# One core, three blocks: the values' product of windowed attention by blocks of 64 keys, its normalisation for the first sequence at the product's eviction, and the next sequence's first scores ahead of the low-rank stage

## The chip, the cores and the metric

The kernel runs on one core of a Trainium2 chip. The metric is the device time of one execution in microseconds, smaller is better. The engines are named as in the profile: PE (TensorE, matrix products and transposes), PEld (its weight loads), DVE (VectorE), ACT (ScalarE), POOL (GpSimd), SP (the queue that issues the DMAs). All operands stay in SBUF; PE writes to PSUM, eight banks of 512 float32 columns, from which DVE and ACT copy ("evict").

## The reference

Four sequences (`batch`) of 576 positions pass through three blocks.

```python
# 1 attention: 8 heads of width 64, window of 128 keys, linear bias
scores = q @ k.T / 8 + slope_h * -|i - j|          # only where 0 <= i - j < 128
attn = exp(scores - max); attn = attn / (sum(attn) + 1e-9)
x = concat_heads(attn @ v)                          # [4, 576, 512]
# 2 low rank mix over positions, then a feed-forward block (hidden 2048)
u = x + ((x.T @ U) @ V).T                           # rank 32, over the 576 positions
x = u + relu(u @ w_ch1) @ w_ch2
# 3 spatial gating
h = relu(x @ w_in); a, b = halves of h
b = layernorm(b); b = w_spatial @ b + b_spatial[:, None]
out = (a * b) @ w_out
```

The inputs U, V and the weight matrices come as 64-bit words of float64 values; the kernel takes them apart into float32 on the chip ("bit unpacking").

## The kernel before, in words

**Attention** is done for one sequence `b` and a pair of heads at a time (`heads`, 16 pairs in all). The 576 queries are cut into nine tiles `t` of 64; both heads of the pair stand in the 128 partitions, and a tile sees at most 192 keys. The steps of a pair:

1. scores on PE (L577, 18 products, in two groups of six and three tiles) into the PSUM ring `sc`;
2. on DVE, for each tile, the bias added and the row's negative maximum taken in one instruction (L589), result to SBUF `p`;
3. on ACT `exp` with the row sums (L594);
4. on DVE one add and one reciprocal for all nine tiles (L599, L601), then nine normalisations `p = p * rinv` (L607 on POOL or L609 on DVE, the planner takes the engine);
5. on PE transposes of `p`, 128x128 each (L616). The keys are cut at 0, 64, 192, 320, 448 (`CH`): a chunk `c` of keys is needed by up to four tiles (`TR`), which makes 17 transposes in five PSUM buffers, evicted to `ph` (L317 on ACT, L318 on DVE);
6. on PE the values' product (L639): 14 matrix products, seven per head, the two heads in the two column halves of the array, with 64 to 256 moving columns each (1088 per head), into two buffers for the query ranges 0 to 320 and 320 to 576; two copies to `u` (L317, L318).

After the fourth pair of a sequence: `u` is transposed (L659), mixed with U (L675), multiplied with V (L687), and added to `u` by eight DVE instructions (L692).

**The feed-forward block** goes over the hidden width in four quarters (`PARTS`) of four chunks of 128. Each operand is split into two float32r parts, so a product is three passes (L460 to L462 and L497 to L499). The first quarter's weights are loaded and unpacked during attention (`part_of_hidden`, DVE L362 to L369, ACT L356, POOL L384), eight of them. With them `NB` = 5 "early" groups of 256 tokens run on PE between the pieces of attention of sequences 1 to 3; all other token groups are "late", 512 tokens at a time (1024 tokens of the first quarter, then all 2304 for each other quarter). **The third block** follows; it is not touched.

**The order** on every engine is made by a planner (`Plan`): each step is a task with an estimated cost, a priority (pairs in order; weights by `K["w0"] + K["w0s"] * c`) and its dependencies, including those of the buffer rings; it lists tasks by the earliest possible start and the priority, and the engines run this list in order. A ring (`Ring`) hands out buffers in turn, in the order in which the Python code asks for them, so code that is written earlier gets its buffer earlier. `qr`, `kr` (queries, keys) have two buffers each, so a pair's load waits for the scores of the pair before the last. The attention's buffers (`att`) are given up for the late ones when all attention is done (`end_att`).

## Time and profile before

| | us |
|---|---|
| median of 3 runs (761.59 to 763.09) | 763.0 |
| the profiled execution | 763.91 |
| its span, first to last instruction | 762.1 |
| PE busy | 735.4 (96%) |
| DVE busy | 414.4 (54%) |
| ACT busy | 318.5 (42%) |
| POOL busy | 268.4 (35%) |

The profile is one execution, of one core. Busy time of PE counts a matrix product from its issue to its modelled end, and products overlap; so a duration there is latency, and the distance between the starts of two instructions is what one costs in a stream. Rows of DVE and ACT overlap by some 0.08 us for the same reason. A float32 product appears as two records, since it goes in two passes. The granted clock is a share of the full 2.4 GHz; the other level is 1.2 GHz.

### The profile page before, as it was taken

The numbers are of one execution on the slowest core, as the hardware profiler recorded it, in microseconds if no ns is written. First come the engines' busy times: TensorE is split into PE (matmuls) and PEld (weight loads), VectorE is DVE, ScalarE is ACT, GpSimd is POOL, SyncE is SP. The second block draws the span as 40 slices with busy tenths as digits, with TensorE's granted clock in tenths as the row PEclk, the third lists the DMA queues.
The fourth block names the chain that finished last, engine by engine and source line by source line (L and its number), as shares of the span: only waits on it lengthen the run. The fifth ranks groups of instructions, "written<-read, shape, count | busy, mean of one in ns | idle before, by whom it ended". The sixth has DMA issues, their size and how long they took to land.

```text
span 762.1 us, 13056 instructions
## 1 busy us (share of the span) xinstructions
PE 735.4 (96%) x4988; PEld 633.0 (83%) x4988; DVE 414.4 (54%) x1077; ACT 318.5 (42%) x856; POOL 268.4 (35%) x347
## 2 busy tenths in 40 slices
PE   6788999999989999999999999999999999999998
PEld 5567888888867888889888888888999899899897
DVE  5999767587499852225992164122685505415220
ACT  5867657485543432124541233122454333332322
POOL 1252231110455652124762136152386206115021
PEclk9999999999999999999999999999999999999999
DMA  6855213120424200006000030000310010100102
GB/s 210 261 174 174 91 32 110 50 79 2 138 99 139 83 1 1 0 1 221 1 0 1 1 112 0 1 1 0 111 48 1 15 43 1 42 28 1 55 2 69
DMA packets 28834, 45.70 MB, mean 60 GB/s; under 512 B 4964, under 2 KB 18020, under 8 KB 28772
## 3 DMA queue, kind: packets, MB, share of 16 engines
q1 hardware_dynamic: 28772, 44.87, 18.3%
q8 instruction: 39, 0.64, 0.4%
q14 instruction: 23, 0.19, 0.1%
HBM read 40.14 MB, written 4.72 MB: 59 GB/s over the span
## 4 chain that ended last, share of the span: by engine, by line
PE 87%; DVE 9%; ACT 1%; DMA 1%; issue 1%; SPq 0%; POOL 0%; ACTq 0%; DVEq 0%; POOLq 0%
PE sc L497 5%; PE sc L499 5%; PE sc L498 5%; PE at L460 5%; PE at L462 5%; PE at L461 5%; PE at L616 4%; PE acc L497 3%; PE at L639 3%; PE acc L499 3%; PE acc L498 3%; PE f L460 3%; PE at L791 3%; PE at L790 3%; PE at L789 3%; PE f L461 3%
## 5 line engine op out<-in xcount | busy, mean ns | idle before, releaser
L434 POOL TENSOR_TENSOR x<-u,xc 128x64 fp32r<-128x64 f32 (+5 forms) x108 | 92.9, 895 | 134.2 <-ACT xc L431 132.9
L469 DVE SCALAR_TENSOR_TENSOR h<-at,h 128x512 fp32r<-128x512 f32 (+1 forms) x51 | 32.7, 642 | 95.6 <-ACT h L467 95.6
L467 ACT ACTIVATE h<-at 128x512 fp32r<-128x512 f32 (+1 forms) x51 | 28.6, 560 | 125.0 <-PE at L462 124.9
L594 ACT ACTIVATE p<-p,nmax 128x192 f32<-128x192 f32 (+1 forms) x144 | 61.5, 432 | 8.8 <-DVE nmax L589 8.8
L616 PE MATMUL at<-ident,p 128*128 128x128 f32 x272 | 42.2, 300 | 5.8 <-DVE p L609 4.5
L589 DVE CUSTOM_DVE_ANT_0 p<-sc,bias 128x192 f32<-128x192 f32 (+1 forms) x144 | 39.9, 327 | 14.2 <-PE sc L577 14.0
L577 PE MATMUL sc<-kr,qr 64*64 64x192 f32 (+2 forms) x576 | 34.3, 335 | 11.9 <-DMA kr<-in_kT 4.6
L460 PE MATMUL at<-xc,wb 128*128 128x512 f32 (+1 forms) x120 | 44.2, 368 | 0.0
L497 PE MATMUL sc<-h,wb 128*128 128x512 f32 (+1 forms) x120 | 44.1, 368 | 0.0
L498 PE MATMUL sc<-h,wb 128*128 128x512 f32 (+1 forms) x120 | 44.1, 368 | 0.0
L462 PE MATMUL at<-x,wb 128*128 128x512 f32 (+1 forms) x120 | 44.1, 368 | 0.0
L461 PE MATMUL at<-xc,wb 128*128 128x512 f32 (+1 forms) x120 | 44.1, 368 | 0.0
L499 PE MATMUL sc<-h,wb 128*128 128x512 f32 (+1 forms) x120 | 44.1, 368 | 0.0
L384 POOL TENSOR_TENSOR wa<-st,wa 128x512 fp32r<-128x512 f32 x24 | 32.6, 1366 | 32.4 <-ACT wa L317 22.4
L616 PEld LDWEIGHTS at<-ident,p 128*128 128x128 f32 x272 | 33.7, 152 | 12.2 <-issue 4.1
L804 POOL TENSOR_TENSOR u<-y,u 128x576 fp32r<-128x576 f32 x16 | 24.0, 1517 | 53.6 <-ACT u L802 53.6
L469 DVE SCALAR_TENSOR_TENSOR h<-f,h 128x512 fp32r<-128x512 f32 (+1 forms) x27 | 17.8, 659 | 42.9 <-ACT h L467 42.8
L384 POOL TENSOR_TENSOR wb<-st,wb 128x512 fp32r<-128x512 f32 x20 | 30.7, 1546 | 28.3 <-ACT wb L317 28.3
L431 ACT CAST xc<-u 128x64 fp32r<-128x64 f32 (+5 forms) x108 | 38.3, 437 | 3.8 <-PE at L687 3.8
L577 PEld LDWEIGHTS sc<-kr,qr 64*64 64x64 f32 x576 | 22.1, 141 | 19.1 <-issue 15.7
L467 ACT ACTIVATE h<-f 128x512 fp32r<-128x512 f32 (+1 forms) x27 | 15.4, 571 | 53.2 <-PE f L462 52.1
L497 PE MATMUL acc<-h,wa 128*128 128x256 f32 (+1 forms) x108 | 35.9, 332 | 1.5 <-DVE y L507 1.2
(327 smaller groups left out, 2274.1 us busy)
## 6 DMA issues: line engine op xcount, KB each, us to landing
wa<-in_w SPq DMA_DIRECT2D x16, 512.0 KB, 5.4
wb<-in_w SPq DMA_DIRECT2D x16, 512.0 KB, 5.0
qr<-in_qT SPq DMA_DIRECT2D x16, 288.0 KB, 2.9
kr<-in_kT SPq DMA_DIRECT2D x16, 288.0 KB, 3.4
vr<-in_v SPq DMA_DIRECT2D x16, 256.0 KB, 2.8
wa<-in_w_in SPq DMA_DIRECT2D x8, 512.0 KB, 3.6
out<-h SPq DMA_DIRECT2D x15, 256.0 KB, 2.0
wb<-in_w_out SPq DMA_DIRECT2D x4, 512.0 KB, 4.3
```

Of the source, the lines that this page charges most:

```text
L384: P.add("POOL", pool_tt(k * c), lambda: nc.gpsimd.tensor_tensor(out=b[:, 1], in0=st.ap(), in1=f32(b[:, 0]), op=ALU.subtract), r=[st, b.par ...
L434: nc.gpsimd.tensor_tensor(out=tl[il][:, o : o + m], in0=ub[:, s : s + m], in1=f32(th[ih][:, o : o + m]), op=ALU.subtract)
L460: nc.tensor.matmul(o, wt[:, 0, k], a[ia], start=k == 0, stop=False)
L461: nc.tensor.matmul(o, wt[:, 1, k], a[ia], start=False, stop=False)
L462: nc.tensor.matmul(o, wt[:, 0, k], l[il], start=False, stop=k == 3)
L469: P.add("DVE", dve(per * n), lambda f1=f1, hh=hh, hl=hl: nc.vector.scalar_tensor_tensor(out=hl.ap(), in0=f1.ap(), scalar=0.0, in1=f32(hh.a ...
L497: nc.tensor.matmul(o, wt[:, 0, 0, c], hh[:, j], start=i == 0 and x == 0, stop=False, skip_group_check=True)
L498: nc.tensor.matmul(o, wt[:, 1, 0, c], hh[:, j], start=False, stop=False, skip_group_check=True)
L499: nc.tensor.matmul(o, wt[:, 0, 0, c], hl[:, j], start=False, stop=i == len(wts) - 1, skip_group_check=True)
L577: nc.tensor.matmul(s[o : o + 64, c0 : c0 + k1 - k0], qr[d, 64 * t : 64 * t + 64], kr[d, k0:k1], start=True, stop=True, skip_group_check=True)
L594: nc.scalar.activation(out=o(), in_=o(), func=AF.Exp, scale=-1.0, bias=nmax[:, sl, t : t + 1], accum_out=sums[:, sl, t : t + 1])
L616: P.add("PE", 0.109, lambda pt=pt, t=t, half=half, blk=blk: nc.tensor.transpose(pt[:, blk * 128 : blk * 128 + 128], p[:, t, half * 128 : h ...
```

## The change

1. **Values' product by 64-key blocks.** A slot of `p` is now 128 columns wide, 13 slots (`NP`) in place of 9 x 256 columns. For tile `t` the last 128 keys stand in one slot (`MAIN`) and the 64 keys before them in half of another (`REST`), so 13 transposes in four PSUM buffers (`GROUPS`, `SLOTS`) take the place of 17 in five; the evictions fall from 2176 to 1664 columns for each pair. The product is 32 matrix products of 64 moving columns: first eight tiles with all 128 rows (two heads in two column halves), then eight with 64 rows in quarters of the array; even and odd tiles go to two PSUM banks of 320 and 256 columns. The values lie in chunks of 128 keys; the zeroed buffers `v0` go.
2. **First sequence** (`plain`, `pn=1`). Its nine normalisations per pair go. In their place POOL makes `dg`, an identity times `rinv` (128x576); PE multiplies it with ones (four products, L659 of the new file), which brings `rinv` to the layout of the output; two ACT copies bring that to SBUF `r`; and the two copies of the product to `u` become two DVE multiplications with `r`. The other three sequences keep the nine normalisations.
3. **Next scores first.** `heads` is cut in two: loads, scores, maxima and `exp` of the next sequence's first pair are asked for ahead of `low_rank`.
4. **Numbers.** `qr`, `kr` get three buffers, `NB` goes from 5 to 6 early groups (1536 tokens; 768 of the first quarter are left for late groups, as 512 and 256), the first quarter's weights get earlier priorities (`w0` 8 to 7, `w0s` 1.23 to 0.6). V is unpacked in a 128x288 layout in place of 128x576 and spread to its four copies by four DMAs from SBUF to SBUF.

```diff
+GROUPS = [(2, 3), (4, 5), (6, 7), (8, 0, 1)]
...
-    r_qr, r_kr, r_vr, r_v0 = Ring(in_att, "qr", 2), Ring(in_att, "kr", 2), Ring(in_att, "vr", 3), Ring(in_att, "v0", 3)
-    r_ph = Ring(in_att, "ph", 6)
+    r_qr, r_kr, r_vr = Ring(in_att, "qr", K["nq"]), Ring(in_att, "kr", K["nq"]), Ring(in_att, "vr", 3)
+    r_ph = Ring(in_att, "ph", 2)
...
-        single(v32, [(0, stacked(block(V, 0, RANK, 0, S), 4))], 1, S, prio_v, None, early_v)
+        single(v4, [(0, stacked(block(V, 0, RANK, q * n, q * n + n), 2), slice(64 * q, 64 * q + 64)) for q in range(2)],
+               1, n, prio_v, None, early_v)
...
+            if plain:
+                dg = r_d.new([128, 9, D], F32)
+                P.add("POOL", pool_tt(S), lambda: nc.gpsimd.tensor_tensor(
+                    out=dg.ap(), in0=eye.ap().broadcast_to([128, 9, D]),
+                    in1=rinv[:, sl, :9].rearrange("p (t o) -> p t o", o=1).broadcast_to([128, 9, D]), op=ALU.mult),
+                    r=[rinv.part(sl), eye.part(0), eye.part(1)], w=[dg], prio=p0 + 4)
+            else:
...
+            for g, (s0, s1) in enumerate(SLOTS):
+                pt = tp.new([128, s1 - s0, 128], F32)
+                for n_ in range(s0, s1):
+                    ts = [t for t in range(9) if n_ in (MAIN.get(t), REST.get(t))]
+                    P.add("PE", 0.109, lambda pt=pt, n_=n_, s0=s0: nc.tensor.transpose(
+                        pt[:, n_ - s0], p[:, n_ * 128 : n_ * 128 + 128], ident), ...)
+                copy(engines("e", "ACT"), 128 * (s1 - s0), lambda s0=s0, s1=s1: x[:, s0:s1], pt.ap, PSUM, ...)
...
+                            if where is MAIN:
+                                rows, c = slice(0, 128), (t - 1) // 2
+                            else:
+                                rows, c = slice(64 * e, 64 * e + 64), (t - 2 * e) // 2
...
+                                nc.tensor.matmul(os_[e][j * 64 : j * 64 + 64, k], vr[rows, j, c], x[rows, where[t], swap : swap + 64],
+                                                 start=(e, j) not in started, stop=last, skip_group_check=True)
...
+            if plain:
+                for e in range(2):
+                    P.add("DVE", dve(D * (5 - e)), lambda e=e: nc.vector.tensor_tensor(
+                        out=view(e), in0=os_[e].ap(), in1=r[:, e::2], op=ALU.mult), r=[r.part(e), os_[e]], w=[ub.part(e)], prio=p0 + 9)
...
-            heads(b, pair)
+            (heads(b, pair) if pair or not b else ahead)()
...
+        if b < B - 1:
+            ahead = heads(b + 1, 0)
         low_rank(b, xts)
...
-K = dict(parts=(4, 4, 4, 4), flex='xeht', cp=0, wp=0, low=6, w0=8, w0s=1.23, nb=5, evac=40.0, nst=3, d0=7, d0s=0.91, lowd=5)
+K = dict(parts=(4, 4, 4, 4), flex='xeht', cp=0, wp=0, low=6, w0=7, w0s=0.6, nb=6, evac=40.0, nst=3, d0=7, d0s=0.91, lowd=5, nq=3, pn=1)
```

How the order changes, at three places. On DVE, behind the first pair's `exp`: the first pair of the first sequence and the beginning of the second pair, before (`p_77`, `p_81` are the two buffers `p`; L609 normalises, L589 takes the maxima):

```order
L599 TENSOR_SCALAR rinv<-sums 128x9
L601 RECIPROCAL rinv<-rinv 128x9
L609 TENSOR_SCALAR p_77<-p_77,rinv 128x64
L609 TENSOR_SCALAR p_77<-p_77,rinv 128x128
L609 TENSOR_SCALAR p_77<-p_77,rinv 128x192 x7
L589 ISA p_81,nmax<-sc,bias 128x64
```

and the same place of the changed kernel (`p_86` the second buffer, L613 the maxima):

```order
L327 COPY ph<-at 128x384
L559 MEMSET u_127 64x32
L624 TENSOR_SCALAR rinv<-sums 128x9
L626 RECIPROCAL rinv<-rinv 128x9
L613 ISA p_86,nmax<-sc,bias 128x64
```

The nine normalisations are gone from between the reciprocal and the next pair's maxima, and two evictions of transposed tiles stand ahead of the reciprocal.

On PE, the second pair of the second sequence, before (L616 transposes, L639 the values' product, L659 the transposes of `u`, L577 scores; `v_533` is a buffer `v0`):

```order
L616 MATMUL at<-ident,p_81 128x128 x2
L639 MATMUL at<-ph,v_533 64x64 x2
L639 MATMUL at<-ph,v_533 64x128 x2
L639 MATMUL at<-ph,vr 64x256 x2
L639 MATMUL at<-ph,vr 64x128 x4
L639 MATMUL at<-ph,vr 64x256 x2
L639 MATMUL at<-ph,vr 64x128 x2
L659 MATMUL at<-ident,u 128x128 x4
```

and in the changed kernel (L602 scores, L648 transposes, L686 the values' product, L713 the transposes of `u`):

```order
L602 MATMUL sc<-kr,qr 64x64 x2
L602 MATMUL sc<-kr,qr 64x128 x2
L602 MATMUL sc<-kr,qr 64x192 x8
L648 MATMUL at<-ident,p_86 128x128 x12
L686 MATMUL at<-ph,vr 64x64 x32
L713 MATMUL at<-ident,u 128x128 x10
```

One product of 32 steps with 64 columns stands in place of 14 in six rows, behind 13 transposes (one is further up) in place of 17.

On DVE, where the early groups end and the weights of the second quarter are unpacked, before (`st` are weights; L469 makes the second part of a hidden chunk, which PE waits for):

```order
L362 TENSOR_SCALAR st<-st 128x512
L363 TENSOR_SCALAR st<-st 128x512
L366 SCALAR_TENSOR_TENSOR st<-wb,st 128x512
L362 TENSOR_SCALAR st<-st 128x512
L369 SCALAR_TENSOR_TENSOR st<-wb,st 128x512
L363 TENSOR_SCALAR st<-st 128x512
L469 SCALAR_TENSOR_TENSOR h<-at,h 128x512
```

and in the changed kernel, from the first weight on (L372 to L379 unpack, L517 adds to `y`, L479 makes the hidden chunk's part):

```order
L372 TENSOR_SCALAR st<-st 128x512
L373 TENSOR_SCALAR st<-st 128x512
L376 SCALAR_TENSOR_TENSOR st<-wb,st 128x512
L517 TENSOR_TENSOR y<-acc,u 128x128 x4
L379 SCALAR_TENSOR_TENSOR st<-wb,st 128x512
L372 TENSOR_SCALAR st<-st 128x512
L479 SCALAR_TENSOR_TENSOR h<-f,h 128x512
```

The same passes come first, but the chunk behind them now belongs to the sixth early group: on PE, 72 products of early groups follow the last low-rank stage in place of 30.

## Rows read from the trace of the kernel before

**Rows 1.** By stretch: us, busy PE, PEld, DVE, ACT, POOL (x count), granted clock, DMA, GB/s.

```profile
0.00:47.00 47.00, 35.12 (x400) 27.11 (x400) 36.01 (x149) 31.64 (x105) 9.05 (x31) 0.96 0.74 234
47.00:80.00 33.00, 26.64 (x304) 21.07 (x297) 31.75 (x123) 25.29 (x91) 14.57 (x20) 0.95 0.50 155
80.00:201.00 121.00, 120.56 (x1357) 102.89 (x1356) 80.84 (x321) 68.71 (x240) 19.89 (x45) 1.00 0.18 53
201.00:216.00 15.00, 11.07 (x62) 9.29 (x62) 11.95 (x21) 8.28 (x18) 13.54 (x14) 1.00 0.85 300
```

**Rows 2.** Timeline of DVE, first sequence: start, us, instructions, [idle before <- releaser].

```profile
11.14 2.06 DVE L609 TENSOR_SCALAR p<-p,rinv 128x64 f32<-128x64 f32 x9
...
22.56 1.00 DVE L609 TENSOR_SCALAR p<-p,rinv 128x192 f32<-128x192 f32 x4
...
25.38 2.06 DVE L609 TENSOR_SCALAR p<-p,rinv 128x64 f32<-128x64 f32 x9
...
35.86 3.07 DVE L609 TENSOR_SCALAR p<-p,rinv 128x64 f32<-128x64 f32 x9
```

**Rows 3.** Timeline of DVE: the bit unpacking, a narrow and a wide pass.

```profile
9.30 0.33 DVE L366 SCALAR_TENSOR_TENSOR u<-raw,u 128x160 uint32<-128x160 uint32 x1
...
28.09 0.75 DVE L366 SCALAR_TENSOR_TENSOR v<-raw,v 128x576 uint32<-128x576 uint32 x1
```

**Rows 4.** Timeline of DVE: first of eight low rank adds, and what follows them.

```profile
46.88 0.46 DVE L692 TENSOR_TENSOR u<-sc,u 128x288 f32<-128x288 f32 x1 [0.51 <-PE at L687]
...
49.81 0.21 DVE L589 CUSTOM_DVE_ANT_0 p<-sc,bias 128x64 f32<-128x64 f32 x1
```

**Rows 5.** Timeline of DVE: evictions of transposed tiles, 512 and 384 columns.

```profile
...
15.52 0.69 DVE L318 COPY ph<-at 128x512 f32<-128x512 f32 x1 [1.42 <-PE at L616]
16.13 0.35 DVE L589 CUSTOM_DVE_ANT_0 p<-sc,bias 128x192 f32<-128x192 f32 x1
...
22.08 0.56 DVE L318 COPY ph<-at 128x384 f32<-128x384 f32 x1
```

**Rows 6.** Timeline of PE: a transpose of the first sequence that waits.

```profile
36.26 1.30 PE L616 MATMUL at<-ident,p 128*128 128x128 f32 x5 [2.58 <-DVE p L609]
```

**Rows 7.** Timeline of POOL: five normalisations, 768 columns in all.

```profile
20.54 2.05 POOL L607 TENSOR_TENSOR p<-p,rinv 128x64 f32<-128x64 f32 x5 [3.23 <-DVE rinv L601]
```

**Rows 8.** Timeline of PE: one pair of heads of the second sequence.

```profile
87.37 1.80 PE L616 MATMUL at<-ident,p 128*128 128x128 f32 x15
88.92 0.36 PE L497 MATMUL acc<-h,wa 128*128 128x256 f32 x1
...
89.60 0.28 PE L499 MATMUL acc<-h,wa 128*128 128x256 f32 x1
89.72 0.38 PE L616 MATMUL at<-ident,p 128*128 128x128 f32 x2
90.03 0.56 PE L639 MATMUL at<-ph,v 128*64 128x64 f32 x8
90.42 1.69 PE L639 MATMUL at<-ph,vr 128*64 128x256 f32 x20
92.04 0.66 PE L659 MATMUL at<-ident,u 128*128 128x128 f32 x4
```

**Rows 9.** Groups of PE, 80 to 200 us: count | busy us, mean ns | idle before.

```profile
L616 PE MATMUL at<-ident,p 128*128 128x128 f32 x168 | 23.2, 276 | 0.2 <-DVE p L609 0.2
```

**Rows 10.** Timeline of PE, where early groups end and late ones begin.

```profile
202.99 0.36 PE L497 MATMUL acc<-h,wa 128*128 128x256 f32 x1 [1.23 <-DVE y L507]
...
205.94 0.39 PE L460 MATMUL at<-xc,wa 128*128 128x512 f32 x1
206.17 0.40 PE L461 MATMUL at<-xc,wa 128*128 128x512 f32 x1
...
214.72 0.50 PE L499 MATMUL acc<-h,wa 128*128 128x512 f32 x1 [2.69 <-DVE h L469]
```

**Rows 11.** Timeline of DVE: a weight pass ahead of that wait.

```profile
212.59 1.48 DVE L363 TENSOR_SCALAR st<-st 128x512 uint32<-128x512 uint32 x1
```

More of the change, by code (lines that the diff above doesn't have):

```diff
@@ L37 @@
 ]
-TR = [
-    [(t, int(t <= 2 * c), i) for i, t in enumerate(range(2 * c - 1, 2 * c + 3)) if 0 <= t <= 8]
-    for c in range(5)
-]
-RANGES = [(0, 320), (320, 576)]
-PV = [
-    [(0, 0, 0, 0), (0, 1, 2, 64), (1, 0, 2, 64), (2, 0, 1, 192)],
-    [(2, 1, 2, 0), (3, 0, 2, 0), (4, 0, 1, 128)],
-]
-CH = [(0, 64)] + [(64 + 128 * i, 128) for i in range(4)]
+GROUPS = [(2, 3), (4, 5), (6, 7), (8, 0, 1)]
+MAIN, REST, AT, NP = {}, {}, {}, 0
+SLOTS = []
+for group in GROUPS:
+    SLOTS.append((NP, NP + (4 if len(group) == 3 else 3)))
+    for t in group:
+        if t % 2 == 0 and t:
+            MAIN[t], REST[t], AT[t] = NP, NP + 1, 128 * NP
+            NP += 2
+        elif t == 0:
+            REST[t], AT[t] = NP, 128 * NP
+            NP += 1
+        else:
+            MAIN[t] = NP
+            AT[t] = 128 * NP - (64 if t > 1 else 0)
+            if t > 1:
+                REST[t] = NP - 1
+            NP += 1
+CH = [(i, 128) for i in (0, 128, 256, 384, 448)]
+TOK = [(0, 64)] + [(64 + 128 * i, 128) for i in range(4)]
 def bias_table():
@@ L343, in single, with load @@
         words = []
-        for k0, src in srcs:
-            part = raw.part(k0 if bits else None)
+        for k0, src, *at in srcs:
+            rows = at[0] if at else slice(0, 128)
+            part = raw.part((k0, rows.start) if bits else None)
             words.append(part)
-            def load(k0=k0, src=src):
-                o = raw[:, k0 : k0 + src.shape[-2]]
+            def load(k0=k0, src=src, rows=rows):
+                o = raw[rows, k0 : k0 + src.shape[-2]]
                 nc.sync.dma_start(out=o.rearrange("p k c t -> p k (c t)") if bits else o, in_=src)
-            P.dma(128, src.shape[-2] * src.shape[-1], load, w=[part], prio=prio if early is None else early)
+            P.dma(rows.stop - rows.start, src.shape[-2] * src.shape[-1], load, w=[part], prio=prio if early is None else early)
         if not bits:
@@ L580, in heads @@
             P.add("PE", 4 * max(sum(64 * min(t + 1, 3) for _, t, _ in tiles if t % 2 == o) for o in range(2)) / 2400 + 0.1,
-                  score, r=[qr, kr], w=list(s.values()), prio=p0 + 1, mode="quarters of scores")
+                  score, r=[qr, kr], w=list(s.values()), prio=p0 + 1, mode="quarters")
             for _, t, _ in tiles:
@@ L612, in heads @@
-        ph = []
-        for c in range(5):
-            pt, x = tp.new([128, 512], F32), r_ph.new([128, 512], F32)
-            for t, half, blk in TR[c]:
-                P.add("PE", 0.109, lambda pt=pt, t=t, half=half, blk=blk: nc.tensor.transpose(
-                    pt[:, blk * 128 : blk * 128 + 128], p[:, t, half * 128 : half * 128 + 128], ident),
-                    r=[p.part(t), p.part("zero")], w=[pt], prio=p0 + 5)
-            cs = slice(TR[c][0][2] * 128, TR[c][-1][2] * 128 + 128)
-            copy(engines("e", "ACT"), cs.stop - cs.start, lambda x=x, cs=cs: x[:, cs], lambda pt=pt, cs=cs: pt[:, cs], PSUM,
-                 r=[pt], w=[x], prio=p0 + 6)
-            ph.append(x)
@@ L624, in heads @@
-        ub = u[b][pair]
-        for (qa, qb), steps in zip(RANGES, PV):
-            o = tp.new([128, qb - qa], F32)
-            def pv(o=o, steps=steps):
-                for step, (c, b0, b1, oc) in enumerate(steps):
-                    for j in range(2):
-                        if b1 == 0:
-                            n, m = 64, ph[c][:, 128 + 64 * j : 192 + 64 * j]
-                        else:
-                            n = 128 * (b1 - b0)
-                            m = ph[c].ap().rearrange("k (p a c) -> k p a c", p=2, a=4)[:, b0:b1]
-                            m = m[:, :, 0::3] if j else m[:, :, 1:3]
-                        nc.tensor.matmul(o[j * 64 : j * 64 + 64, oc : oc + n], vr[:, j, c - 1] if c else v0[:, j], m,
-                                         start=step == 0, stop=step == len(steps) - 1, skip_group_check=True)
-            P.add("PE", 4 * sum(128 * (b1 - b0) or 64 for _, b0, b1, _ in steps) / 2400 + 0.05, pv,
-                  r=[vr, v0.part(0), v0.part(1)] + [ph[c] for c in sorted({c for c, *_ in steps})], w=[o], prio=p0 + 8, mode="columns")
-            copy(engines("x", "ACT"), qb - qa, lambda qa=qa, qb=qb: ub[:, qa:qb], o.ap, PSUM,
-                 r=[o], w=[ub.part(qa)], prio=p0 + 9)
@@ L647, in turned @@
+        return rest
     def turned(b, half):
@@ L687, in up @@
                     nc.tensor.matmul(o.ap(), th[d], v32[d, sl], start=True, stop=True)
-            P.add("PE", 4 * 288 / 2400 + 0.1, up, r=[th, v32], w=outs, prio=p0 + 0.1, mode="quarter rows")
+            P.add("PE", 4 * 288 / 2400 + 0.1, up, r=[th] + list(v32.parts.values()), w=outs, prio=p0 + 0.1, mode="quarter rows")
             for pair, o in enumerate(outs):
@@ L751, in tile_kernel @@
     ws = []
[L752 removed]
+    for c, (s0, n) in enumerate(TOK):
         st = r_raw.new([128, S], F32)
```

105 lines of the change are left out of this document (76 added, 29 removed).

## The prediction

> **What bounds the kernel now.** I read the busy time by stretch first [rows 1]. It shows two regimes. From 80 to 201 us PE is busy 120.56 of 121 us at a granted clock of 1.00: there a microsecond taken from PE's stream is a microsecond of the program. Before that it is not so: from 47 to 80 us DVE is busy 31.75 of 33 us and PE idle 6.4, and from 0 to 47 us DVE is busy 36.0 us, nearly all that the wait for the first scores leaves, while ACT has 31.6 and POOL 9.1. That DVE is what PE waits for shows in a transpose of the fourth pair, which stands 2.58 us until DVE's normalisation is done [rows 6]. Between 201 and 216 us PE has a third kind of time, 3.9 us idle, at the change from early to late groups. The rest of the program is PE at its limit again and the change does not touch it but for the sizes of three groups. So the change is priced three times: by DVE's work up to 80 us, by PE's work from there to 201, and by the waits at 201 to 216.
>
> **First sequence, by DVE.** Taken away: 31 normalisations on DVE, in four stretches of 2.06, 1.00, 2.06 and 3.07 us [rows 2]: 8.2 us. Two copies of the product to `u`: the evictions cost 0.61 us for 512 columns (distance of two starts) and 0.48 for 384 [rows 5, 2], about 1 ns a column, so 320 and 256 columns are 0.42 and 0.35: 0.8 us. V's unpacking has half the columns. Its wide pass is 0.75 us for 576 columns where U's is 0.33 for 160 [rows 3], so 288 columns are 0.46, 0.29 less in each of two wide passes: 0.6 us; the two narrow ones I leave out.
>
> Added to DVE: eight multiplications with `r`, 320 and 256 columns. The eight low rank adds have 288 each, the same mean, a PSUM and an SBUF operand too, and take 2.93 us from the first to what follows them [rows 4]: 2.9 us. The evictions: in the new order DVE has nine of 384 and two of 512 columns in the first sequence, where it had six of 512, one of 384 and one of 256; that is 5.5 against 4.5 us: 1.0 us. One more eviction of `xt` falls to DVE with 512 in place of 256 columns: 0.3 us.
>
> Sum: -8.2 - 0.8 - 0.6 + 2.9 + 1.0 + 0.3 = **-5.4 us** of DVE. Since DVE stays near full until 80 us, I take it as that much less time to the point where PE is full. Above, the bound is nothing gained, if the first sequence's latency takes DVE's place (rival A). Below, it is -8, since PE's 6.4 idle us up to 80 are not all DVE's work in series, and the earlier weights and the earlier scores of the next sequence can fill some of them.
>
> What is added off DVE in that stretch: PE's four products with `ones` (320 columns per quarter; at the product's 1.81 ns a column, worked out below, 0.6 us per pair), POOL's `dg` (POOL needs 2.05 us for 768 columns in five pieces [rows 7], so 576 are about 1.5 us), ACT's two copies (0.8 us), while ACT loses more than that in evictions. All three engines have room in rows 1 and I cost them at nothing. If that cover is gone, it is rival A. The third queue buffer and the four DMAs that spread V stand on SP's queue: they wait there for DVE's unpacking, with a weight and the next sequence's queries behind them; those are needed some 10 us later, so nothing.
>
> **PE's stream, 80 to 201 us.** 168 transposes run there [rows 9], 17 a pair, so ten of the sixteen pairs. For a pair [rows 8]: 15 transposes take 1.55 us to the next instruction's start, 0.103 each. Four fewer are **-0.41 us**. The old product takes 2.01 us to the next instruction's start and has 1088 columns per head, the two heads side by side; its first eight records hold 64 + 128 columns and take 0.39 us, so the other 896 take 1.62 us, 1.81 ns a column with 0.04 us left over. The new one has 13 steps of 64 columns in series, 832 columns (eight of all rows, then five, as the even tiles' five quarters hide the odd tiles' three): 1.55 us at best. At worst each step costs what the first eight records leave for their 64 columns, 0.39 - 0.23 = 0.16 us, so 2.08 us, and 0.10 more for the change of shape inside the product from all rows to half of them: two transposes ahead of the product take 0.31 us where two of 0.103 would take 0.21, so a change of shape is 0.10. That is 2.2 us. I take 1.70, near the lower end, because 0.04 + 832 x 1.81 ns + 0.10 is 1.65 and I leave 0.05 for the shorter steps: **-0.31 us** (from +0.2 to -0.46). A pair: -0.72 us; ten pairs: **-7.2 us** (from -2.1 to -8.7). The six earlier pairs save it too, but in DVE's stretch, where it hides.
>
> The Trainium skill, "TensorEngine Tiling (Array Packing)", section "Tiling Modes", says that a change of tiling mode drains the engine; the trace agrees with the 0.10 us of two transposes ahead of the product. By a free change the sum would be 1 us lower.
>
> **Group sizes.** A sixth early group and a late one of 256 take the place of one late group of 512, 96 products of it. One of 256 tokens is 0.12 us from start to start [rows 8], one of 512 is 0.23 [rows 10]: 96 x (2 x 0.12 - 0.23) = **+1.0 us** (0 to +2).
>
> **The change from early to late groups.** PE waits 1.23 us for DVE's add to `y` and 2.69 us for a hidden chunk's part [rows 10]; the latter stands on DVE behind a weight pass that takes 1.48 us while POOL works [rows 11]. The same passes come first in the new order, but 72 early products (8.6 us at 0.12) lie behind the last low-rank stage in place of 30 (3.6 us). I take off a part, **-1.5 us** (0 to -3.9). The time until the second quarter's weights are needed shrinks by about the group that went, 10 us; this is part of rival C.
>
> **The sum.** -5.4 - 7.2 + 1.0 - 1.5 = -13.1 us. Against the profiled execution's 763.9 us that is 750.8; the median of the runs shown is 0.9 us lower than that execution. I say 750.5 us. The granted clock averages 0.96 and 0.95 in the first two stretches [rows 1], so PE ran there at the lower of its two levels for a short time (with 1.2 of 2.4 GHz granted, 0.96 of 47 us means 3.8 us of it, half of them lost). Whether the new waits call that again I cannot tell: 2 us either way.
>
> **The rivals.**
>
> A. *The first sequence doesn't get shorter* (18%). The normalisation now runs over four engines: DVE's reciprocal, POOL's `dg`, PE, ACT, then DVE again, and PE, in order, holds everything behind its products with `ones`. For it: about 1.5 + 0.6 + 0.8 us and four hand-overs follow the reciprocal, and the multiplication stands in DVE's order behind the next pair's maxima. Against it: the transposes no longer wait for the normalisation, and the product comes after transposes and evictions that take as long. Then the -5.4 us go: 756 us.
>
> B. *More than the sum* (20%). PE's idle time between 47 and 80 us goes by half (3 us) since weights and scores come earlier, and all of the 3.9 us at 201 to 216 goes: another 5.5 us, 745 us. For it: more early work lies ready for PE. Against: DVE is 96% busy there, and that work needs DVE first.
>
> C. *Something late is late* (8%). The second quarter's weights, or the chunk parts that DVE makes among them, come after PE asks for them, since ten microseconds less lie ahead and DVE's passes triple beside POOL [rows 11]. One or two more such waits of 2.7 us [rows 10] make 754 to 757 us.
>
> D. *The short steps show their weight loads: slower* (4%). Every step of the new product loads new weights for 64 columns, 26 loads in series per head. PE's weight loads in 80 to 201 us are busy 102.89 us for 1356, 0.076 us each [rows 1]. If none hides, a pair's product is 1.55 + 26 x 0.076 = 3.5 us, 1.1 us more than is saved in both steps; ten pairs cost 11 us, and the sum is -5.4 + 11 + 1.0 - 1.5 = +5 us: 769 us. It decides from a product of about 3.0 us on, where ten pairs eat the other terms. Against it: the old product's first eight records have loads of the same width at 64 and 128 columns, four deep, and take 0.39 us, which has room for 0.04 us beside the columns, not for 0.30 [rows 8]. The Trainium skill, "TensorE: Matmul & The Clock Gate", section "Part 3: Packing small matmuls — row/col tiling", says that weight loads overlap products in flight only where the row groups differ; by it the eight steps with all rows would show their loads. The 0.39 us disagree with that.
>
> **How the numbers follow.** Forecast 50%, A 18%, B 20%, C 8%, D 4%. The range of the likeliest alone: -2.1 to -8.7 in the pairs and 0 to -3.9 at the change give 748 to 757, with the clock 747 to 758. For 8 in 10 I take in B, and A and C with a little room: 743 to 759 us. No change means within 0.2%, 1.5 us, about what a measurement of this kernel tells. All cases but D are faster, and C or A with the bad end of the product come near to nothing: faster 0.91, same 0.03, slower 0.06.
>
> **What would show it.** In the new profile: the values' product 1.6 to 1.8 us from its first start to the next instruction's (over 2, and the largest term falls); 13 transposes in about 1.35 us; DVE's last low rank add of the first sequence near 46 us, with the nine maxima of the next pair already done, where now it ends at 49.81 with none of them done; PE full from about 74 us; less than 3 us of waits between the last low-rank stage and the second quarter. Wrong would be the forecast if PE waited for the products with `ones`, or if the stretch before PE is full were as long as now.

## The result, and the profile after

The changed kernel takes **749.58 us** (median of 4 runs, 748.04 to 750.48) where the kernel before takes 762.75 (4 runs, 761.59 to 763.09): ratio **0.9828**, 95% interval 0.9807 to 0.9848. The prediction said 750.5. The profiled execution of after is the fastest of its four (748.04 us, span 746.3), that of before the slowest of its own; so the two profiles differ by 15.8 us of span where the medians differ by 13.2.

Three numbers of a page split a span: the span, PE's busy time and the mean granted clock. What the clock took is (1 - clock) x span. PE's busy time less that is PE's work at full clock. Span less busy is the time without PE: its waits, and some 8 us of beginning and end. (In a stretch that is both half-clocked and full of waits this books a little too much to the clock.)

| us | span | PE's work | the clock | without PE |
|---|---|---|---|---|
| before | 762.1 | 732.4 | 3.0 | 26.7 |
| after | 746.3 | 721.6 | 3.7 | 21.0 |
| difference | -15.8 | -10.8 | +0.7 | -5.7 |

So in these two executions two thirds came from a shorter stream on PE and one third from fewer waits. Where the waits went is read from three stretches of both kernels (columns as in [rows 1]: length, busy PE, PEld, DVE, ACT, POOL, granted clock, DMA share, GB/s). Before:

```profile
4.60:80.00 75.40, 61.70 (x696) 48.10 (x697) 67.76 (x271) 55.45 (x194) 21.00 (x31) 0.95 0.64 203
80.00:185.00 105.00, 104.56 (x1182) 88.89 (x1181) 73.92 (x305) 63.93 (x230) 19.52 (x44) 1.00 0.21 61
185.00:240.00 55.00, 51.07 (x344) 43.16 (x343) 41.81 (x74) 24.46 (x48) 26.13 (x25) 1.00 0.30 102
```

and after:

```profile
4.60:80.00 75.40, 64.41 (x978) 50.71 (x979) 69.11 (x272) 57.83 (x211) 27.94 (x33) 0.95 0.66 217
80.00:185.00 105.00, 104.27 (x1592) 92.06 (x1590) 71.36 (x301) 57.62 (x209) 14.67 (x29) 1.00 0.18 52
185.00:240.00 55.00, 53.62 (x351) 48.56 (x350) 47.66 (x82) 26.65 (x57) 31.68 (x29) 1.00 0.39 130
```

Length less PE's busy time: up to 80 us 13.70 became 10.99, from 80 to 185 us 0.44 became 0.73, from 185 to 240 us 3.93 became 1.38.

**The pair's stream.** What answers to [rows 8], on PE's timeline (start, us, instructions, [idle before <- releaser]):

```profile
81.42 1.88 PE L686 MATMUL at<-ph,vr 128*64 128x64 f32 x64
83.23 0.55 PE L648 MATMUL at<-ident,p 128*128 128x128 f32 x3
```

The product, 64 records (32 steps in two passes), takes 1.81 us to the next instruction's start, where it took 2.01. In the single records behind this row a step of the first kind (128 rows, the two heads side by side, two passes) takes 0.117 us, which is 64 columns at the 1.81 ns of the old product: the weight loads are hidden. Thirteen such steps would be 1.52 us. What stands above that lies at the start (0.11 us to the second pass), at the change to half the rows (0.09 more than a pass) and at the way out (0.15 from the last record to the transposes). The transposes:

```profile
119.54 1.15 PE L648 MATMUL at<-ident,p 128*128 128x128 f32 x9
120.44 0.36 PE L470 MATMUL f<-x,wa 128*128 128x256 f32 x1
...
121.96 0.60 PE L648 MATMUL at<-ident,p 128*128 128x128 f32 x4
122.49 0.87 PE L602 MATMUL sc<-kr,qr 64*64 64x192 f32 x12
```

Nine and four: 0.90 + 0.53 = 1.43 us, where 15 and two took 1.86. A pair is 0.43 + 0.20 = 0.63 us shorter.

**The first sequence's end.** DVE, what answers to [rows 4]:

```profile
42.19 0.35 DVE L613 CUSTOM_DVE_ANT_0 p<-sc,bias 128x192 f32<-128x192 f32 x1
...
43.41 0.45 DVE L746 TENSOR_TENSOR u<-sc,u 128x288 f32<-128x288 f32 x1
...
45.96 0.44 DVE L746 TENSOR_TENSOR u<-at,u 128x288 f32<-128x288 f32 x1
46.33 0.56 DVE L624 TENSOR_SCALAR rinv<-sums 128x9 f32<-128x9 f32 x1
```

The low rank adds begin at 43.41 and what follows them at 46.33, in place of 46.88 and 49.81, and the nine maxima of the next pair (the last at 42.19) stand ahead of them.

**Waits of PE** behind that:

```profile
42.37 0.48 PE L741 MATMUL sc<-v,th 32*128 32x288 f32 x1 [1.82 <-issue]
...
48.42 0.56 PE L602 MATMUL sc<-kr,qr 64*64 64x192 f32 x8 [1.84 <-DVE nmax L613]
...
62.24 0.56 PE L602 MATMUL sc<-kr,qr 64*64 64x192 f32 x8 [2.81 <-DVE nmax L613]
```

L741 (the low rank products) stood 1.82 us, put down to "issue": it needs the `sc` buffers that the next pair's scores hold until DVE has read them, which is at 42.2 to 42.5 (shown by e4 below). This wait is new. Those for DVE's maxima, 1.84 and 2.81 us, are not: before had 4.4 us of them in four waits. What went is the waiting of transposes for the normalisation, on before's list of waits (us in total, times, longest):

```profile
PE at L616 <- DVE p L609: 4.5, 5, 2.6
PE at L616 <- POOL p L607: 0.8, 1, 0.8
```

Neither has a counterpart in after, and none of PE's waits there stands at the products with ones.

**Early to late**, what answers to [rows 10]. PE:

```profile
202.37 0.28 PE L507 MATMUL acc<-h,wa 128*128 128x256 f32 x1
202.49 0.28 PE L508 MATMUL acc<-h,wa 128*128 128x256 f32 x1
204.15 0.38 PE L509 MATMUL acc<-h,wa 128*128 128x256 f32 x1 [1.38 <-DVE h L479]
```

and DVE beside it:

```profile
202.54 0.95 DVE L373 TENSOR_SCALAR st<-st 128x512 uint32<-128x512 uint32 x1
203.41 0.68 DVE L479 SCALAR_TENSOR_TENSOR h<-f,h 128x512 fp32r<-128x512 f32 x1
```

Of the two waits, 1.23 and 2.69 us, one is gone and one is 1.38: still a hidden chunk's part (L479) behind a weight pass.

### The profile page after: what moved, and what is told of

Read it like the earlier page. It is cut to its first block, busy times and chain, and to the rows that moved or that the text cites. A ratio compares the mean times of both kernels' runs of the same rounds, so it can differ in the third digit from the quotient of the medians.

```text
span 746.3 us, 14284 instructions
## 1 busy us (share of the span) xinstructions
PE 725.3 (97%) x5628; PEld 632.7 (85%) x5628; DVE 406.5 (54%) x1066; ACT 309.5 (41%) x845; POOL 268.5 (36%) x328
## 4 chain that ended last, share of the span: by engine, by line
PE 91%; DMA 3%; DVE 3%; ACT 1%; SPq 1%; issue 1%; ACTq 0%
PE sc L507 5%; PE sc L509 5%; PE sc L508 5%; PE at L470 5%; PE at L471 5%; PE at L472 5%; PE f L470 4%; PE acc L507 3%; PE f L472 3%; PE f L471 3%; PE acc L509 3%; PE acc L508 3%; PE at L648 3%; PE at L846 3%; PE at L847 3%; PE at L845 3%
## 5 line engine op out<-in xcount | busy, mean ns | idle before, releaser
L444 POOL TENSOR_TENSOR x<-u,xc 128x192 fp32r<-128x192 f32 (+5 forms) x108 | 91.5, 880 | 133.9 <-ACT xc L441 131.6
L479 DVE SCALAR_TENSOR_TENSOR h<-at,h 128x512 fp32r<-128x512 f32 (+1 forms) x51 | 31.9, 626 | 96.2 <-ACT h L477 96.2
L394 POOL TENSOR_TENSOR wa<-st,wa 128x512 fp32r<-128x512 f32 x24 | 36.4, 1530 | 31.9 <-ACT wa L326 31.9
L613 DVE CUSTOM_DVE_ANT_0 p<-sc,bias 128x192 f32<-128x192 f32 (+1 forms) x144 | 40.3, 326 | 10.3 <-PE sc L602 10.1
L602 PE MATMUL sc<-kr,qr 64*64 64x192 f32 (+2 forms) x576 | 34.0, 336 | 10.6 <-DVE nmax L613 4.7
L470 PE MATMUL at<-xc,wb 128*128 128x512 f32 (+1 forms) x120 | 44.2, 368 | 0.0
L479 DVE SCALAR_TENSOR_TENSOR h<-f,h 128x512 fp32r<-128x512 f32 (+1 forms) x29 | 18.9, 651 | 44.5 <-ACT h L477 44.3
L394 POOL TENSOR_TENSOR wb<-st,wb 128x512 fp32r<-128x512 f32 x20 | 31.0, 1560 | 27.9 <-ACT wb L326 27.9
L507 PE MATMUL acc<-h,wa 128*128 128x256 f32 (+1 forms) x124 | 39.5, 319 | 0.0
L509 PE MATMUL acc<-h,wa 128*128 128x256 f32 (+1 forms) x124 | 37.2, 300 | 1.4 <-DVE h L479 1.4
L472 PE MATMUL f<-x,wa 128*128 128x256 f32 (+1 forms) x124 | 37.9, 306 | 0.0
L441 ACT CAST xc<-u 128x192 fp32r<-128x192 f32 (+5 forms) x108 | 37.4, 430 | 0.3 <-PE at L741 0.3
L508 PE MATMUL acc<-h,wa 128*128 128x256 f32 (+1 forms) x124 | 37.1, 299 | 0.0
```

Of the source, the lines that this page charges most:

```text
L394: P.add("POOL", pool_tt(k * c), lambda: nc.gpsimd.tensor_tensor(out=b[:, 1], in0=st.ap(), in1=f32(b[:, 0]), op=ALU.subtract), r=[st, b.par ...
L444: nc.gpsimd.tensor_tensor(out=tl[il][:, o : o + m], in0=ub[:, s : s + m], in1=f32(th[ih][:, o : o + m]), op=ALU.subtract)
L470: nc.tensor.matmul(o, wt[:, 0, k], a[ia], start=k == 0, stop=False)
L472: nc.tensor.matmul(o, wt[:, 0, k], l[il], start=False, stop=k == 3)
L479: P.add("DVE", dve(per * n), lambda f1=f1, hh=hh, hl=hl: nc.vector.scalar_tensor_tensor(out=hl.ap(), in0=f1.ap(), scalar=0.0, in1=f32(hh.a ...
L507: nc.tensor.matmul(o, wt[:, 0, 0, c], hh[:, j], start=i == 0 and x == 0, stop=False, skip_group_check=True)
```

## The experiments

All ratios are to the kernel before on the same chip, where it measured 762.25 (e1 to e4), 764.22 (e5 to e8) and 762.49 us (e9 to e12); after stands at 0.9828, so 0.001 is 0.76 us. Where two runs are compared below without a word on it, it is by these ratios; after's interval is 0.9807 to 0.9848, and only e1, e2, e5, e7, e9 and e10 lie clear of it. In the expectations of e1 to e8 "theory" is the prediction's account: the product and transposes by PE's stream, the first sequence by DVE's time. From e9 on "theory now" is the one formed after e7: DVE's freed time and the earlier weights pay only together.

| kernel | ratio | 95% | span | PE's work | clock | without PE |
|---|---|---|---|---|---|---|
| e1 product alone | 0.9905 | 0.9888 to 0.9923 | 752.9 | 720.8 | 3.8 | 28.3 |
| e2 first sequence normalised | 0.9884 | 0.9867 to 0.9900 | 752.4 | 721.1 | 3.8 | 27.5 |
| e3 five early groups | 0.9841 | 0.9825 to 0.9858 | 748.8 | 720.8 | 5.2 | 22.8 |
| e4 low rank first | 0.9858 | 0.9842 to 0.9874 | 749.4 | 724.7 | 1.5 | 23.2 |
| e5 three more transposes | 0.9941 | 0.9925 to 0.9958 | 758.2 | 728.2 | 5.3 | 24.7 |
| e6 two sequences at the eviction | 0.9849 | 0.9832 to 0.9867 | 750.0 | 723.8 | 3.8 | 22.4 |
| e7 old weight priorities | 0.9902 | 0.9886 to 0.9917 | 753.3 | 723.1 | 3.8 | 26.4 |
| e8 two query buffers | 0.9806 | 0.9789 to 0.9823 | 747.0 | 720.5 | 6.7 | 19.8 |
| e9 product + earlier weights | 0.9996 | 0.9976 to 1.0015 | 760.7 | 718.6 | 12.2 | 29.9 |
| e10 product + first sequence | 0.9952 | 0.9934 to 0.9971 | 757.3 | 723.3 | 8.3 | 25.7 |
| e11 weights closer | 0.9845 | 0.9820 to 0.9870 | 749.2 | 720.9 | 5.2 | 23.1 |
| e12 weights from 5 | 0.9848 | 0.9822 to 0.9875 | 750.2 | 720.6 | 5.3 | 24.3 |

**e1: the product's change** (with V's unpacking in 288 columns and the fewer evictions, which are part of its code) **and nothing else.** `low_rank` and the next scores in the old order, and

```diff
-K = dict(..., w0=7, w0s=0.6, nb=6, ..., nq=3, pn=1)
+K = dict(..., w0=8, w0s=1.23, nb=5, ..., nq=2, pn=0)
```

> The product by 64-key blocks (with its 13 transposes, and V unpacked in 288 columns) in the order and with the numbers of before: all sequences normalised as before, 5 early groups, two buffers, old weight priorities, low rank ahead of the next scores. Theory (PE's stream from 80 us on pays for what the pair costs): ten pairs save 0.41 us in transposes and 0.20 us in the product (2.00 to 1.81), 6 us, and some 1 us of evictions and unpacking in DVE's stretch: 755 to 757 us against 762.75. Rival (the product is no gain, what is won comes from the first sequence and the order): 761 to 764 us.

754.75 us, 7.5 less than before: at the edge of the theory's range, and far from the rival's. Between the two profiles PE's work is down by 11.6 us, 1.6 us came back as waits and 0.8 at the clock:

```profile
4.60:80.00 75.40, 60.43 (x968) 47.56 (x968) 68.13 (x279) 54.73 (x198) 24.79 (x37) 0.95 0.65 206
80.00:185.00 105.00, 102.71 (x1498) 89.44 (x1496) 72.13 (x293) 59.19 (x214) 19.77 (x40) 1.00 0.19 59
```

Up to 80 us PE lacks 14.97 in place of 13.70, and from 80 to 185 us 2.29 in place of 0.44. A shorter stream asks for DVE's results earlier. That the six pairs in DVE's stretch save nothing is not what the rows show: the low rank adds of the first sequence are over at 47.0 us in place of 49.8. How much of that is PE's and how much DVE's, which has fewer evictions and half of V's columns here, the run does not tell.

**e2: the first sequence normalised ahead of its transposes** (`pn=0` in after).

> The changed kernel with the first sequence normalised as the other three (nine normalisations a pair, no dg, no products with ones). Theory (DVE sets the length of the first 80 us): 8.2 us of normalisations come back, 2.9 us of multiplications become 0.8 us of copies on DVE or none: 754 to 756 us against 749.6. Rival (the first sequence is bounded by latency or by other engines): 748 to 751 us.

753.42 us: 0.0056 or 4.3 us over after, just under the theory's range and over the rival's. PE's work is the same; the waits are not:

```profile
4.60:80.00 75.40, 60.54 (x928) 47.20 (x924) 68.22 (x280) 55.62 (x203) 25.66 (x35) 0.95 0.63 205
...
185.00:240.00 55.00, 51.40 (x338) 46.86 (x338) 49.07 (x82) 25.00 (x49) 32.76 (x27) 1.00 0.30 103
```

Up to 80 us 14.86 in place of 10.99 (3.9 us), and 3.60 in place of 1.38 from 185 us on. The longest new one, 3.15 us at 10.53, is put down to the load of the second pair's keys; in after PE does not stand there, since it runs the first pair's transposes (8.06 to 10.78 us), which in e2 come behind the normalisation, at 13.50. So part of the gain is PE's order at the very start, and not DVE's sum of work.

**e3: five early groups** (`nb=5` in after).

> The changed kernel with five early groups in place of six. Theory (a sixth group costs 1.0 us of shorter products and saves about 1.5 us of waits at the change to late groups): 749 to 751 us, with a wait of 2 to 4 us between the last low rank stage and the second quarter. Rival (the sixth group is what keeps PE full during attention, which now has less work of its own): 753 us or more, with idle time of PE between 80 us and the end of attention.

750.57 us, inside the theory's range, 1.0 over after, with intervals that overlap: the sixth group is worth about nothing either way. In the table 0.8 us less of PE's work stands against 1.8 us more of waits.

**e4: the next sequence's scores behind low rank, as before.**

```diff
-            (heads(b, pair) if pair or not b else ahead)()
+            heads(b, pair)()
...
-        if b < B - 1:
-            ahead = heads(b + 1, 0)
```

> The changed kernel with the next sequence's first scores asked for after the low rank stage, as before. Theory (the order only swaps one wait of PE for another, 1.8 us at the low rank products against the scores behind the adds): 748.5 to 751 us, and no wait over 1 us at the low rank products of the first sequence. Rival (the earlier maxima fill DVE at the junction): 752 to 754 us, with two or more us of idle PE between the low rank products and the first scores of the second sequence.

751.64 us, 2.3 over after (the intervals just touch), between the two. The first low rank product then stands 0.37 us for ACT's `th`:

```profile
39.99 0.51 PE L741 MATMUL sc<-v,th 32*128 32x288 f32 x1 [0.37 <-ACT th L326]
```

So the 1.82 us of after were the `sc` buffers. Low rank was 2 us earlier, and the kernel still no faster: the early scores are worth at least the wait that they cause.

**e5: three more transposes per pair**, 16 as against 13, into a part of the PSUM buffer that nobody reads.

```diff
+                if s1 - s0 < 4:
+                    P.add("PE", 0.109, lambda pt=pt, s0=s0: nc.tensor.transpose(
+                        pt[:, 3], p[:, s0 * 128 : s0 * 128 + 128], ident), ...)
```

> The changed kernel with three transposes more in each pair (16 in place of 13), written to a spare part of their PSUM buffer and read by nobody; evictions as before. Theory (PE's stream pays in full from about 80 us on, and DVE hides it earlier): 48 transposes, of which 27 to 30 behind 80 us, at 0.103 us: 2.8 to 3.1 us more than 749.6, 752 to 753 us. Rival 1 (PE has slack in the pairs): 749 to 750.5 us. Rival 2 (PE pays in all 16 pairs): 754.5 us.

759.59 us: 8.6 over after, more than the theory and both rivals. PE's work is up by 6.6 us, 0.14 for each of 48, the time without PE by 3.7 and the clock's by 1.6. But the edit did more than add transposes: the list of tasks came out in another order. At the end of the first sequence the rest of the next sequence's first scores now stands ahead of the transposes of `u`, and PE waits there for maxima:

```profile
39.01 0.56 PE L602 MATMUL sc<-kr,qr 64*64 64x192 f32 x8 [2.56 <-DVE nmax L613]
41.35 2.39 PE L716 MATMUL at<-ident,u 128*128 128x128 f32 x10 [1.25 <-ACT y L326]
```

So the low rank adds of the first sequence end at 51.7 us, 5.3 later than in after, where twelve transposes more are 1.2 us. All 48 at 0.103 are 4.9 us of the 8.6. The run shows that PE has no slack for them; it does not price a transpose, nor say in which pairs it costs.

**e6: two sequences normalised at the eviction** (`pn=2`).

> The changed kernel with the second sequence normalised at the product's eviction as well. Theory (DVE is the limit from 47 to 80 us too, where 22 normalisations keep it busy 6.9 us, and one stretch of nine takes 3.8 us, ahead of a wait of PE of 2.8 us): DVE loses 4 us net, PE gets 4 x 0.65 us of products with ones: 746 to 748 us. Rival (PE, which is full in most of the second sequence, pays the 2.6 us and gains nothing): 751 to 753 us.

752.37 us, 1.6 over after, inside the rival's range: no gain. PE's work is 2.2 us more and the time without PE 1.4 more, though DVE is busy 4.9 us less in all (401.6 as against 406.5).

**e7: the old weight priorities in after.**

```diff
-K = dict(..., w0=7, w0s=0.6, ...)
+K = dict(..., w0=8, w0s=1.23, ...)
```

> The changed kernel with the first quarter's weights at the old priorities (8 + 1.23 c). Theory (DVE does the same work in another order; with weights later PE has less to fill waits with behind 47 us): 750.5 to 753 us. Rival (DVE then serves the maxima earlier and the wait of 2.8 us goes): 747 to 749 us.

756.17 us, 5.6 over after: the theory's direction, and more than the 0.9 to 3.4 that it allowed. This number, for which the prediction has no term, is as large as that of the first sequence.

```profile
4.60:80.00 75.40, 64.58 (x1042) 49.45 (x1042) 68.39 (x279) 58.38 (x214) 22.98 (x27) 0.95 0.66 211
80.00:185.00 105.00, 102.09 (x1510) 89.07 (x1510) 73.34 (x290) 62.07 (x220) 22.64 (x43) 1.00 0.24 75
185.00:240.00 55.00, 50.02 (x316) 44.59 (x317) 50.63 (x78) 21.30 (x39) 33.68 (x28) 1.00 0.20 67
```

Up to 80 us PE waits no more than in after (10.82). The time is lost later: 2.91 from 80 to 185 and 4.98 from 185 us on. When the weights come is read from POOL, which finishes each of the eight (L394). After:

```profile
66.51 6.61 POOL L394 TENSOR_TENSOR wa<-st,wa 128x512 fp32r<-128x512 f32 x3 [3.07 <-ACT wa L326]
```

e7:

```profile
82.04 1.47 POOL L394 TENSOR_TENSOR wa<-st,wa 128x512 fp32r<-128x512 f32 x1 [5.27 <-ACT wa L326]
...
89.16 1.29 POOL L394 TENSOR_TENSOR wa<-st,wa 128x512 fp32r<-128x512 f32 x1 [0.33 <-ACT wa L326]
```

The last is ready at 73.1 us in after and at 90.5 in e7. One of PE's new waits there, 0.91 us at 75.57, names POOL's `wa` itself; by 100 us PE has run 96 of the early groups' products in e7 and 148 in after.

**e8: two query buffers** (`nq=2`).

> The changed kernel with two buffers each for queries and keys. Theory (loads land well ahead of the scores, as in the kernel before, where PE waited for a load only at the start): 749 to 751 us. Rival (with the scores asked for earlier, the load behind them comes too late): 752 us or more, with waits of the scores for a DMA in the first 100 us.

748.95 us; the interval overlaps after's. The third buffer brings nothing; whether it costs something stays open.

**e9: the product and the earlier weights** (e1 with `w0=7, w0s=0.6`).

> The product's change and the earlier weight priorities (7 + 0.6 c), and nothing else of the change: the first sequence keeps its normalisations, five early groups, two query buffers, scores behind low rank. Before is 1; the product alone measured 0.9905 (some 755 us), the whole change 0.9828 (750). Theory now (DVE's time freed in the first sequence and the earlier weights pay only together, since DVE is full there): earlier weights without the freed time push the attention back by what they bring, so little over the product alone, 0.988 to 0.992 (753.5 to 756.5 us). Rival 1 (the weights' dates alone carry it): 0.983 to 0.985 (749.5 to 751). Rival 2 (they only push the attention back): over 0.993.

762.83 us, no better than before and 6.9 us (by the ratios; 8.1 by the medians) worse than the product alone: rival 2, and the theory was too kind. The weights are ready early (the eighth at 75.8 us, 86.4 in e1), but the table shows 12.2 us gone to the clock, 8.4 more than in e1, while waits and work together differ by 0.6. Of the 12.2, 5.1 are lost behind the last low rank, where e1 loses none; most of the rest lies in three stretches at the lower clock up to 80 us (about 11, 45 and 65.5), where e1 has one (47 to 54). The stretches behind the last low rank:

```profile
198.60:205.50 6.90, 6.71 (x14) 4.01 (x15) 2.76 (x5) 5.48 (x13) 6.90 (x9) 0.51 0.96 333
205.50:212.30 6.80, 3.93 (x18) 2.88 (x17) 6.80 (x6) 1.82 (x4) 6.40 (x5) 1.00 0.88 324
212.30:216.00 3.70, 3.70 (x11) 2.91 (x10) 3.63 (x7) 1.20 (x2) 1.23 (x1) 0.54 0.01 2
```

and the first late products:

```profile
198.66 0.77 PE L470 MATMUL at<-xc,wa 128*128 128x512 f32 x1 [0.97 <-ACT xc L441]
...
211.42 0.50 PE L509 MATMUL acc<-h,wa 128*128 128x512 f32 x1 [2.87 <-DVE h L479]
```

With the weights early, PE runs the five early groups between the pieces of attention, which is thereby later (last low rank at 197.3 us, 190.6 in e1), and none of their products is left as filler behind it (e1 has 48, before 30). There PE waits for the late groups' tokens (0.97 us), runs them at 0.51 of the clock, and waits 2.87 us for a hidden chunk's part.

**e10: the product and the first sequence at the eviction** (e1 with `pn=1`).

> The product's change and the first sequence normalised at the product's eviction, and nothing else of the change: old weight priorities (8 + 1.23 c), five early groups, two query buffers, scores behind low rank. Theory now (freed DVE time is worth nothing while the weights come late): as the product alone, 0.989 to 0.992 (754 to 756.5 us), with the low rank adds of the first sequence some 3 us earlier than in the product alone and the weights not. Rival, the prediction's step (DVE's 5.4 us less are the program's): 0.983 to 0.985 (749.5 to 751).

759.21 us, 3.6 us (by the ratios; 4.5 by the medians) worse than the product alone, which neither explanation had; the prediction's step would have made it some 4 better. Yet the step did something:

```profile
4.60:80.00 75.40, 63.84 (x993) 49.57 (x993) 67.76 (x262) 55.98 (x200) 22.43 (x26) 0.93 0.66 209
80.00:185.00 105.00, 101.79 (x1417) 88.43 (x1417) 70.92 (x294) 57.67 (x211) 19.92 (x40) 0.97 0.19 57
185.00:240.00 55.00, 52.99 (x375) 44.51 (x374) 43.70 (x72) 23.68 (x46) 29.11 (x25) 1.00 0.35 121
```

Up to 80 us PE waits 11.56 us in place of e1's 14.97, and the low rank adds end at 44.2 us (47.0 in e1, 49.8 before). But PE waits further on:

```profile
75.82 1.88 PE L686 MATMUL at<-ph,vr 128*64 128x64 f32 x64 [0.68 <-ACT ph L326]
80.15 0.76 PE L648 MATMUL at<-ident,p 128*128 128x128 f32 x4 [2.46 <-DVE p L640]
81.77 0.44 PE L648 MATMUL at<-ident,p 128*128 128x128 f32 x2 [0.85 <-DVE p L640]
```

and what DVE does ahead of these normalisations is unpack weights:

```profile
76.05 0.75 DVE L372 TENSOR_SCALAR st<-st 128x512 f32<-128x512 f32 x2
76.72 0.75 DVE L373 TENSOR_SCALAR st<-st 128x512 uint32<-128x512 uint32 x2
77.39 0.68 DVE L376 SCALAR_TENSOR_TENSOR st<-wa,st 128x512 uint32<-128x512 uint32 x1
...
79.33 3.06 DVE L640 TENSOR_SCALAR p<-p,rinv 128x64 f32<-128x64 f32 x9
```

Seven weight passes from 76.05 on (four in the first two rows) for the late seventh and eighth weight (ready at 81.6 and 85.3 us) stand between the maxima and the nine normalisations at 79.33. PE is busy 3.02 of the 7.00 us from 75 to 82, and from 82 to 89 the granted clock is 0.51:

```profile
75.00:82.00 7.00, 3.02 (x72) 2.36 (x70) 7.00 (x24) 3.70 (x11) 1.45 (x1) 1.00 0.49 146
82.00:89.00 7.00, 6.17 (x79) 5.51 (x78) 2.11 (x5) 1.90 (x4) 1.27 (x1) 0.51 0.02 4
```

Over the whole span e10 waits 2.6 us less than e1. Its loss stands in the other two columns of the table: 4.5 us at the clock, 3.4 of them in the stretch from 82, and 2.5 us of PE's work, which no run explains. Over all runs the clock differs less (a mean of 0.990 in ten runs, 0.993 in five of e1).

**e11, e12: the weights earlier still** (`w0s=0.3`, and `w0=5`, both with two query buffers).

> The whole change with two query buffers (measured 0.9806) and weight priorities 7 + 0.3 c in place of 7 + 0.6 c, so the eight weights come closer behind one another. Theory (a microsecond of earlier weights is feed-forward work for PE's idle stretches up to 80 us; its idle time after the first start is still 13 us): 0.977 to 0.980 (745 to 748 us). Rival (DVE has no more to give there: weight passes put off maxima and low rank, as much as they bring): 0.980 to 0.985 (748 to 752 us).

> The whole change with two query buffers (measured 0.9806) and weight priorities 5 + 0.6 c in place of 7 + 0.6 c, so all eight begin earlier. Theory (as for the closer weights): 0.977 to 0.980 (745 to 748 us). Rival (weights ahead of the first sequence's own work put off its low rank, without which no early group can run): 0.982 to 0.988 (750 to 754 us), with the last low rank add of the first sequence later than 46.4 us by what the weight passes take.

751.09 and 752.0 us: both the rival's, 3.0 and 3.2 over e8, from which they differ in the weights' priorities alone (the intervals just touch). Both lack more than e8 up to 80 us (13.15 and 14.41 us, e8 10.06) and the same behind it. In e12 weight passes now split the low rank adds, which end 2.4 us later than after's:

```profile
46.82 0.44 DVE L746 TENSOR_TENSOR u<-at,u 128x288 f32<-128x288 f32 x1
...
48.03 0.44 DVE L746 TENSOR_TENSOR u<-sc,u 128x288 f32<-128x288 f32 x1
48.40 0.44 DVE L746 TENSOR_TENSOR u<-at,u 128x288 f32<-128x288 f32 x1
```

The dates in after are near the best of those tried. No kernel here is clearly faster than after.

## Why the prediction was right, and where only its sum was

1. **PE's stream** (-7.2 us for ten pairs): the size came out in e1, 7.5 us, by another sum. The product came to 1.81 us and not to 1.70, since its ends and quarter steps take more; per pair 0.63 in place of 0.72, so ten pairs are 6.3 us. The rest of the 7.5 lies where the prediction had nothing: that the six earlier pairs' saving "hides" in DVE's stretch is not borne out, since e1's first sequence ends 2.8 us earlier. Rival D is refuted by the 0.117 us of a step. The Trainium skill, "TensorE: Matmul & The Clock Gate", section "Part 3: Packing small matmuls — row/col tiling", has loads overlap products in flight only where the row groups differ, and by that sentence the steps with all rows would show theirs; this trace disagrees with it, as the 0.39 us of [rows 8] had. (The same section also names loads into a background buffer that run ahead; with that the 0.117 us agree.)
2. **First sequence by DVE** (-5.4 us): the first sequence's end moved by that much (e10: 49.8 to 44.2, 5.6 us), but by luck in its parts: the product alone brings 2.8 of it (47.0 in e1), where the sum charged the product's evictions, less V's columns, with 0.7 us more; the first sequence's step brings the other 2.8, where the sum had 6.1. And it is refuted as a rule. The sentence that fails is "I take it as that much less time to the point where PE is full". e10 has the earlier end and is some 4 us slower than e1. In after it pays: 4.3 us by e2.
3. **"The third queue buffer and the four DMAs ... so nothing"**: right for the buffer (e8). The DMAs were not tried apart.
4. **The earlier weights and scores** had no term, only a mention as the lower bound of the first sequence and in rival B. They are worth 5.6 and, hardly clear of noise, 2.3 us where all the rest is there (e7, e4), and the weights cost 6.9 to 8.1 us where it isn't (e9 beside e1, by ratio or median). This is the largest miss. The three terms beside the product, -5.4 + 1.0 - 1.5, are -5.9 us, and after is 5.9 us under e1: the sum came right since DVE's term, taken whole, stood in for what DVE's time and the weights' dates bring together. That the two are equal is luck.
5. **Group sizes** (+1.0) and **early to late** (-1.5): e3 undoes both, -0.5 in the sum, and shows -1.0, not to be told from zero; its work (0.8 us less) and its waits (1.8 us more) have the two terms' signs and sizes. Against before PE lacks 2.55 us less from 185 to 240.
6. **Rival A** is refuted as it was put: PE waits nowhere at the products with ones. **B** and **C** did not come to pass; what C feared, a late hidden chunk, is the 1.38 us at 204.15. PE was not full from 74 us but from about 72.5; the waits between the last low rank and the second quarter were 1.4 us, under the 3 named.
7. **The arithmetic.** -13.1 from 763.9, less the 0.9 by which the median lies lower, is 749.9; the 750.5 has 0.6 for which no term stands. The range's upper end, 757, adds the bad ends of both terms; by the same rule the lower one would be 747, not 748.

What is shown: with the product in all of them, neither DVE's freed time (e10) nor the earlier weights (e9) gains over e1; each gains where the other stands beside it with the sixth group and the early scores (after against e7 and e2). The mechanism that the rows support: PE needs filler while DVE is its bound, DVE must unpack the filler's weights, and it can do that early only if the first sequence leaves it time. Late weights put the passes among the second sequence's normalisations (e10); early ones without the rest use the filler up before the attention ends (e9). In the profiled executions of both, most of the loss against e1 stands in the clock's column, behind such waits where it was followed.

This mechanism is argued from rows, not shown by a run: the two edits together and nothing else of the rest, on top of e1, were not run. A rival stands beside it: every edit has the planner list all tasks anew, as e5 shows, and nearby numbers move the time by 1 to 3 us (e3, e4, e11, e12), so a part of the 3.6 us of e10 may be the order and not the edit; 6.9 us in e9 and 5.6 in e7 are more than that. What else stays open: which of DVE's time, the sixth group and the early scores repairs e9 (e3 says that the group isn't needed in after), and why PE's work differs by 2 to 3 us between kernels with the same instructions (after 721.6, e4 724.7): stretches at either clock and overlapping records blur it.

## What to carry to other kernels

Freed time on an engine is worth what the next engine can do with it: before pricing it, look for what that engine will run then and whether its operands are there, and price the two edits together. Undoing one edit at a time cost 4.3, 1.0, 2.3 and 5.6 us, 13.2 in all, where e1 and after are 5.9 us apart; only runs with one edit added showed that two of them gain nothing alone. Three numbers of a page (span, PE's busy time, granted clock) tell a shorter stream from fewer waits and from a lower clock. After an edit that changes the order, look first where each stage ends in both traces: in e5 that showed that the edit had moved more than it was meant to.

## What the hardware showed beside that

- The granted clock followed the kernel, with chance beside it: e9's twelve runs had 0.982 to 0.991 (median 0.985), its 21 runs of before 0.986 to 0.996 (median 0.993). At the medians that is 11.4 us lost in e9 and 5.3 in before; the 12.2 and 3.0 of the table are single executions. In e10 the clock stood at 0.51, the lower of its two levels (1.2 and 2.4 GHz), after PE had been busy 3.02 of 7.00 us; in e9 it stood at 0.54 after 3.93 of 6.80 us.
- Steps of 64 columns with the same 128 rows and new weights each time run at 0.117 us, the rate of the wide ones.
- The change from all rows to half of them inside a product took 0.09 us, near the 0.10 that two transposes ahead of the old product had let expect.
